# Hash products in one two-bank PSUM tile, values scaled before they are split, loads with a first allowed time

## The chip, the cores and the metric

The kernel runs on one NeuronCore of one Trainium2 chip. The metric is the device time of one execution in microseconds (us), taken from several runs of the same program; lower is better. A profile is one further execution with the hardware profiler on. Five engines work side by side, each with its own instruction queue that is worked off in order: PE (matrix products), ACT (activations, copies, casts), DVE (vector operations), POOL (vector operations, SBUF only) and SP, which here issues nearly all DMAs.

## The reference

Two batches of eight heads, 768 tokens, head size 64. Attention is masked by a hash: six projections of q and of k are turned into sign bits, and a query sees the keys whose six bits equal its own. The result goes through two feed-forward networks with different gates.

```python
q_bits = (np.einsum('bhsd,dk->bhsk', q, proj) > 0)      # proj: 64 x 6
k_bits = (np.einsum('bhsd,dk->bhsk', k, proj) > 0)
mask = q_bucket[:, :, :, None] == k_bucket[:, :, None, :]
scores = np.where(mask, scale * q @ k^T, -1e9)
attn = softmax(scores)
x = (attn @ v)                       # 1536 tokens x 512
h = x @ w_in1;  x = (h * sigmoid(h)) @ w_out1            # 512 -> 2048 -> 512
h = x @ w_in2;  x = (h - tanh(h)) @ w_out2
```

## The kernel before, in words

**Precision.** Each fp32 product is built from two parts, a rounded high part and a low rest, so a product is three matmuls (high*high, high*low, low*high). Casting to the high part and subtracting to get the low part is most of the work of ACT, DVE and POOL.

**Attention.** There are 16 heads (numbers 0 to 15; 0 to 7 are batch 0) with 6 query tiles of 128 rows each, 96 tiles in all. For a head, a raw tile `r` with q and k is loaded (L372), split into `q1, q2, k1, k2` (L380 to L396), and the hash products go into PSUM (`hash_mm`, L413): two halves of 384 tokens, each into a bank of its own taken from the three to four general banks (`banks`). DVE turns the products into bit rows: for head 0 four instructions that write straight into the operands (`ev0`, L423), for every other head two instructions into a helper tile `hb` (`ev`, L437), from which SP copies the rows by two DMAs (L445, L448) into the operands, where they act as extra rows of the score product, so that a mismatch pushes a score far down.

For a tile: scores (PE, L558) into a two-bank PSUM tile out of `s_slots`, of which there are two until batch 0 is through and one after that; row maximum and eviction (DVE, L562); bias (L567); exp (ACT, L572); then the transpose of the probabilities, in one of two ways. A *direct* tile is transposed by PE in two halves (L586), each evicted into fp16 high (ACT, L595) and low (DVE, L599) parts. Any other tile is cast to fp16 (ACT, L614), its rest is subtracted on POOL (L617), and the pair is transposed by a DMA issued from SP (L620) into `pt`. The knobs `direct` and `direct1` say which share of the tiles of batch 0 and batch 1 is direct: 0.4 and 0.083, which gives 19 and 4 tiles. Then the product with the values (PE, L635 to L637, 18 matmuls).

**Values.** For each batch six row blocks are loaded in three DMAs (L461) and scanned for the largest magnitude (`v_max`, L470, DVE); one PE product spreads it over all partitions (L480), and a power of two `vsc` comes out (L483 to L487). `v_hi` (ACT, L502) writes the scaled fp16 high part, and `v_lo` the rest: one DVE instruction that scales and subtracts (L512), or two on POOL. No value product may start before all twelve pieces are done. The raw values of both batches use the same SBUF slot (`acc_slot`), so the loads of batch 1 wait for the last `v_lo` of batch 0.

**Feed-forward.** Weights are loaded as 64-bit floats, 512 KB a piece (L799), and turned into fp32 on the chip: `c_abs` (ACT), `c_clip` (L834, POOL or DVE), three DVE instructions (L837, L841, L845), a cast (ACT, L849) and a subtraction (L853). Converted weights of the first network are also stored to DRAM (L872) for a second pass. The first network's tokens of batch 0 run interleaved with the attention of batch 1; then come the first network's second half and the second network with seven products in place of eight (L1229) and its output product (L1321). Its weight conversion has the same steps (L1084 to L1105).

**The order.** The order of every queue is written out before the program is built. `Plan.add` takes an engine (or several, with a price for each), a key (a due time) and dependencies; `Plan.order` (L95) is a list scheduler over assumed prices: it takes the work that could start first, and among work within `slack` of that the one with the lowest key. A task with a second or third engine goes there when that would end earlier by more than a bias (`b_...`; 50 or more means never). Keys come from `when(i)` (L330), which gives tile i the time `start + step * i` in batch 0 and a gap and `step1` in batch 1, and from `t_group` for the feed-forward products. A DMA without unmet dependencies may be placed as soon as SP is free in the plan. On the chip each queue runs in the planned order whatever the real durations are: an instruction that is not ready holds up all behind it.

Of the kernel before, what the change touches and what calls it, by code (L numbers as in the profile page):

```python
# [23 lines left out]

KNOBS = dict(start=1.134, step=2.53, gap=9.388, step1=3.92, ffn=3.61, ffn3=2.212, pv=12.257, prep=16.11, hash=8.464,
             slack=0.042, conv=32.734, conv0=53.318, vld=10.124, vmax=13.049, vsplit=16.427, x2=0.269, direct=0.4,
             direct1=0.083, b_qh=1.32, b_qlo=100, b_kup=100, b_vlo=2, b_bi=2.75, b_thi=100, b_shi=0.98, b_slo=100,
             b_xh=1.72, b_xlo=1.56, b_wlo=100, b_clip=-0.24, b_hhi=0.67, k_m=-0.273, k_e=0.107, k_t=1.899,
             k_th=2.064, k_tl=2.019, k_hi=1.332, k_lo=1.98, k_f=3.209, cj=3.559, cl=8.822, ahead=2, emode=1, lmode=1,
             xsets=0, raws=5, vmax1=70.287, ffn2=2.15, xprep=14.912, xprep1=2.896, xk1=2.806, convo=54.917,  # L30
             convh=37.499, fill=14.668, convo0=35.195, convh0=75.173, fill0=45.82, plain=3, cj2=5.837, half=2,
             b_xph=1.92, b_xpl=-0.35, b_cl2=2.16, b_wl2=100, b_sh=100, b_ss=1.98, b_u3=100, b_hh2=1.76, b_hl2=-0.24,
             by=3.547)

# [19 lines left out]
class Task:  # L54
    __slots__ = ("ways", "eng", "fn", "key", "deps", "uses", "takes", "left", "next", "ready", "end", "start", "tail",
                 "opens", "n", "bias", "line")


class Plan:
# [7 lines left out]

    def add(self, eng, cost, fn, key, deps=(), takes=(), uses=(), tail=0.0, port=False, give=None, line=None):
# [17 lines left out]
        t.next, t.end, t.start = [], None, None  # L86
        t.n = len(self.tasks)
        self.tasks.append(t)
        return t
# [113 lines left out]
def lsh_attention_moe_kernel(  # L203
# [116 lines left out]
    def get(h):  # L320
        if h.tile is None:
            h.tile = h.slots[0].make()
        return h.tile
# [35 lines left out]
    for n in range(NHEAD):  # L359
# [47 lines left out]
        if n >= THREE:  # L407
            parts.append(add(("ACT", "POOL", "DVE"), (0.82, 1.84, 0.6), k_up, at + 1, [ld[1], hold], uses=[raw, ops],
                             port=("DVE",), give="kup"))
        hk = [Held(*banks), Held(*banks)]  # L410
        hat = a0 - K["hash"] if n else -45.0

        def hash_mm(n=n, hk=hk, get_ops=get_ops):  # L413
            q1, q2, k1, k2 = get_ops()
            for u in range(2):
                pairs = ((hq1, q1), (hk1, k1), (hk2, k2), (hq2, q2)) if n < THREE else ((hq1, q1), (hk1, k1), (hqk, q2))
                for i, (w, x) in enumerate(pairs):
                    nc.tensor.matmul(out=get(hk[u])[0:82, 0:HS], lhsT=w, rhs=x[:, u * HS:(u + 1) * HS],  # L418
                                     start=(i == 0), stop=(i == len(pairs) - 1))

        hm = add("PE", 1.4 if n < THREE else 1.05, hash_mm, hat, parts + [hash_ready], takes=hk, uses=[ops])
        if n == 0:
            def ev0(u, side, hk=hk, get_ops=get_ops):  # L423
                _, q2, _, k2 = get_ops()
                us = slice(u * HS, (u + 1) * HS)
                ps = get(hk[u])[0:82, 0:HS]
                if side == 0:
                    nc.vector.tensor_scalar(q2[0:18, us], ps[0:18, :], thr[0:18, :], sc[0:18, :],
                                            op0=ALU.is_gt, op1=ALU.mult)
                else:  # L430
                    nc.vector.tensor_scalar(k2[0:18, us], ps[64:82, :], thr[64:82, :], None, op0=ALU.is_gt)
            bits = [add("DVE", 0.64, lambda u=u, s=s: ev0(u, s), hat + 1, [hm], uses=[ops, hk[u]])
                    for u in range(2) for s in range(2)]
        else:
            hb = Held((hb_slot,))

            def ev(u, hk=hk, hb=hb):  # L437
                nc.vector.tensor_scalar(get(hb)[0:82, u * HS:(u + 1) * HS], get(hk[u])[0:82, 0:HS], thr[0:82, :],
                                        sc[0:82, :], op0=ALU.is_gt, op1=ALU.mult)
# [10 lines left out]
            bits = [add("SP", 0.73, f, hat + 2, [e0, e1], uses=[hb, ops], tail=0.18) for f in (bits_q, bits_k)]  # L450
        heads[n] = (ops, get_ops, bits)

    vals = {}
    for b in range(B):
# [5 lines left out]
        def load_v(t, b=b, vr=vr):  # L460
# [42 lines left out]

        def v_lo(e, t, vr=vr, vh=vh, vsc=vsc):
            row = get(vr)[:, t, :]
            src = row.rearrange("p (h d) -> p h d", h=H)
            hi, lo = (x[:, t, :, 0:D] for x in get(vh))
            if e == "POOL":
                nc.gpsimd.tensor_scalar(row, row, vsc, None, op0=ALU.mult)
                nc.gpsimd.tensor_tensor(lo, src, hi, op=ALU.subtract)  # L510
            else:
                nc.vector.scalar_tensor_tensor(lo, src, vsc, hi, op0=ALU.mult, op1=ALU.subtract)  # L512

        out = []
        for t in range(NQ):
            x = add("ACT", 0.72, lambda t=t, f=v_hi: f(t), a0 + K["vsplit"] + t, [t3, vo], uses=[vr, vh])
            out += [x, add(("DVE", "POOL"), (0.745, 2.6), lambda e, t=t, f=v_lo: f(e, t), a0 + K["vsplit"] + 0.5 + t, [x],
                           uses=[vr, vh], port=("DVE",), give="vlo")]
# [236 lines left out]
    for ps_i, (e, fresh, blks) in enumerate(PASSES):  # L755
        pairs = [blks[i:i + 2] for i in range(0, len(blks), 2)]
        accs = {}
        for c in range(NCH):
            base = seq[0]
            wset = []  # L760
            for m in range(2):
# [18 lines left out]
                for j in range(4):  # L780
# [16 lines left out]
                    def load_w(src=src, w_tile=w_tile, fresh=fresh):  # L797
# [3 lines left out]
                    ld = add("SP", 0.35, load_w, kj - K["cl"], ([] if fresh else [stored[ps_i - 1, c, m, j]]),  # L801
                             takes=[w], tail=1.65 if fresh else 0.82)
                    prior = [first_take] if first_take else [ld]
# [11 lines left out]
                    else:  # L815
# [252 lines left out]
    for c in range(NCH):  # L1068
        cb = unit0 + CU * c

        def fetch(m, j, wv, key):
# [20 lines left out]
            def c_clip(e):  # L1092
                ENG[e].tensor_scalar(val().bitcast(F32), val().bitcast(F32), W_MIN, W_MAX, op0=ALU.max, op1=ALU.min)  # L1093

# [12 lines left out]

            ld = add("SP", 0.35, load, key - K["cl"], [], takes=[w], tail=1.65)
            a = add("ACT", 0.65, c_abs, key, [ld, spare] + wv.first[:1], takes=[] if wv.first else [wv],
# [294 lines left out]
```

## Time and profile before

| | |
|---|---|
| median of 3 runs | 745.14 us (742.0 to 747.14) |
| the profiled execution | 746.36 us, span 744.6 us |
| PE busy | 704.2 us, 95% of the span, 5390 matmuls |
| DVE / ACT / POOL busy | 558.3 us / 452.2 us / 504.3 us |
| mean granted TensorE clock | 0.988 of full speed |

The span runs from the first to the last instruction of the profile; the rest of the execution's time lies around it. PE's busy time counts overlapping matmuls once and goes on while a matmul waits in the array, so a busy PE is not one at its peak. DMA share is the mean busy share of the 16 DMA engines and can come out slightly above 1. In rows "x <- y" reads "x was waited for by": the engine and line on the left stood idle until the one on the right was done. SPq is SP's queue.

### The profile page before, as it was taken

To read this page: it belongs to the slowest core of one execution; us is meant where nothing else is said; L and a number is where in the kernel's file an instruction comes from. 1 tells how busy PE (TensorE), PEld (TensorE's weight loads), DVE (VectorE), ACT (ScalarE), POOL (GpSimd) and SP (SyncE) were. 2 spreads that over 40 slices of the span, in tenths; PEclk is the share of its full clock that TensorE was granted. 3 is DMA by queue.
4 is the path that set the end of the run, shared out by engine and by line. 5 is a ranking of instruction groups with operands and counts; after the bars stand their busy time and mean duration, and the time that the engine had idled before them with its cause. 6 is when DMAs were issued, how large, how long until landed. Compare 5 with 4: busy or idle time off the path is not lost.

```text
span 744.6 us, 14192 instructions
## 1 busy us (share of the span) xinstructions
PE 704.2 (95%) x5390; PEld 679.6 (91%) x5390; DVE 558.3 (75%) x1025; ACT 452.2 (61%) x853; POOL 504.3 (68%) x340
## 2 busy tenths in 40 slices
PE   5679888799999999999999999989999999999998
PEld 4569787599999999999999999989999999999997
DVE  5889998798987888986834464888869768775453
ACT  5879998897796984875634344464535445253240
POOL 5757887679699874776942467897897598565120
PEclk9889999999999999999999999999999999999999
DMA  9687899979999997894322322312312202300102
GB/s 355 145 214 136 209 183 219 258 147 241 244 246 235 240 198 208 204 194 115 92 74 84 86 85 85 108 36 64 113 47 88 87 29 70 101 1 1 53 33 85
DMA packets 140447, 100.77 MB, mean 135 GB/s; under 512 B 117439, under 2 KB 119743, under 8 KB 140379
## 3 DMA queue, kind: packets, MB, share of 16 engines
q1 hardware_dynamic: 140090, 99.59, 54.0%
q8 instruction: 42, 0.69, 0.4%
q10 hardware_dynamic: 288, 0.28, 0.1%
q14 instruction: 27, 0.21, 0.1%
HBM read 57.95 MB, written 11.53 MB: 93 GB/s over the span
## 4 chain that ended last, share of the span: by engine, by line
PE 65%; ACT 9%; DVE 7%; POOL 7%; DMA 7%; issue 4%; SPq 0%; POOLq 0%; ACTq 0%; DVEq 0%
PE psm L1321 14%; PE psm L1229 13%; PE psm L906 13%; PE psm L968 11%; PE ps L558 6%; ACT p L572 2%; DMA w<-in_w_in_dram 2%; PE psm L418 2%; POOL wl L810 2%; POOL x L1093 2%; PE pso L635 2%; PE pso L636 1%; PE pso L637 1%; ACT hl L338 1%; DMA w<-in_w_out_dram 1%
## 5 line engine op out<-in xcount | busy, mean ns | idle before, releaser
L617 POOL TENSOR_TENSOR hl<-p,hl 128x768 f16<-128x768 f32 x73 | 121.5, 1666 | 54.7 <-ACT hl L338 42.6
L562 DVE TENSOR_SCALAR_CACHE_REDUCE p<-ps 128x768 f32<-128x768 f32 x96 | 90.4, 952 | 17.7 <-PE ps L558 11.1
L558 PE MATMUL ps<-k,q 128*128 128x384 f32 x384 | 90.7, 363 | 5.7 <-DVE p L562 3.9
L572 ACT ACTIVATE p<-p,bi 128x768 f32<-128x768 f32 x96 | 89.4, 937 | 1.8
L906 PE MATMUL psm<-xh,wh 128*128 128x384 f32 x256 | 86.9, 340 | 1.1 <-DVE p L599 0.7
L968 PE MATMUL psm<-gh,wh 128*128 128x384 f32 x256 | 86.7, 339 | 0.0
L906 PE MATMUL psm<-xl,wh 128*128 128x384 f32 x256 | 86.2, 337 | 0.2 <-DVE xl L677 0.2
L906 PE MATMUL psm<-xh,wl 128*128 128x384 f32 x256 | 86.1, 336 | 0.0
L968 PE MATMUL psm<-gh,wl 128*128 128x384 f32 x256 | 85.7, 335 | 0.0
L968 PE MATMUL psm<-gl,wh 128*128 128x384 f32 x256 | 85.7, 335 | 0.0
L1321 PE MATMUL psm<-gl,wh 128*128 128x384 f32 x256 | 85.6, 334 | 0.0
L1321 PE MATMUL psm<-gh,wh 128*128 128x384 f32 x256 | 85.5, 334 | 0.0
L1321 PE MATMUL psm<-gh,wl 128*128 128x384 f32 x256 | 85.5, 334 | 0.0
L558 PEld LDWEIGHTS ps<-k,q 128*128 128x128 f32 x384 | 67.4, 197 | 8.8 <-DVE p L562 4.6
L810 POOL TENSOR_TENSOR wl<-w,wh 128x512 fp32r<-128x512 f32 x32 | 44.6, 1403 | 37.1 <-ACT wh L806 37.0
L338 ACT CAST hl<-p 128x768 f16<-128x768 f32 x71 | 59.1, 833 | 0.5
L635 PEld LDWEIGHTS <-pt 128*128 128x128 f16 x438 | 40.0, 97 | 15.0 <-DMA pt<-hl 8.1
L635 PE MATMUL pso<-v,pt 128*128 128x65 f16 x438 | 47.8, 195 | 6.2 <-DMA pt<-hl 6.0
L1328 DVE TENSOR_TENSOR acc<-acc,psm 128x384 f32<-128x384 f32 x48 | 26.4, 551 | 33.3 <-PE psm L1321 33.1
L853 POOL TENSOR_TENSOR wl<-wa,wh 128x512 fp32r<-128x512 f32 x32 | 42.1, 1317 | 12.2 <-ACT wh L849 11.9
L924 DVE TENSOR_TENSOR gl<-psm,gh 128x384 fp32r<-128x384 f32 x64 | 35.2, 553 | 19.6 <-ACT gh L338 19.1
L906 PEld LDWEIGHTS psm<-xh,wh 128*128 128x128 f32 x256 | 48.1, 188 | 1.9 <-DVE p L599 1.2
(146 smaller groups left out, 2222.3 us busy)
## 6 DMA issues: line engine op xcount, KB each, us to landing
w<-in_w_in_dram SPq DMA_DIRECT2D x32, 512.0 KB
w<-in_w_out_dram SPq DMA_DIRECT2D x32, 512.0 KB
r<-in_qkT_dram SPq DMA_DIRECT2D x15, 768.0 KB
wi<-wa SPq DMA_DIRECT2D x16, 256.0 KB
wo<-wa SPq DMA_DIRECT2D x16, 256.0 KB
w<-wi SPq DMA_DIRECT2D x16, 256.0 KB
w<-wo SPq DMA_DIRECT2D x16, 256.0 KB
vr<-in_v_dram SPq DMA_DIRECT2D x6, 512.0 KB
```

Source lines behind the costliest of these rows:

```text
L338: nc.scalar.copy(out, in_) if e == "ACT" else ENG[e].tensor_copy(out, in_)
L558: nc.tensor.matmul(out=get(ps)[:, u, 0:HS], lhsT=x[:, t * 128:(t + 1) * 128], rhs=c[:, u * HS:(u + 1) * HS], start=(j == 0), stop=(j == 1))
L562: nc.vector.tensor_scalar(get_p().rearrange("p (c s) -> p c s", c=2), get(ps)[:, :, 0:HS], FLOOR, None, op0=ALU.max, op1=ALU.max, accum_ou ...
L572: nc.scalar.activation(out=get_p(), in_=get_p(), func=ACTF.Exp, scale=0.125, bias=get(bi))
L617: ENG[e].tensor_tensor(get_hl()[:, 1, :], get_p(), get_hl()[:, 0, :], op=ALU.subtract)
L635: nc.tensor.matmul(out=o, lhsT=pt[:, kt, :], rhs=v16[:, kt, h, :], start=(kt == 0), stop=False)
L810: ENG[e].tensor_tensor(ll, w_tile(), hh.bitcast(F32), op=ALU.subtract)
L853: ENG[e].tensor_tensor(ll, get(wa).bitcast(F32), hh.bitcast(F32), op=ALU.subtract)
L906: nc.tensor.matmul(out=ps, lhsT=a[:, k, fs], rhs=b_[blk][:, k, :], start=(k == 0 and j == 0), stop=(k == KD - 1 and j == 2))
L968: nc.tensor.matmul(out=ps, lhsT=a[:, f, ds], rhs=b_.tile[:, f, :], start=(f == 0 and j == 0), stop=(f == F - 1 and j == 2))
L1229: nc.tensor.matmul(out=ps, lhsT=sw[a][:, o, 2 * k + p, :], rhs=xw[b_][:, k, :], start=(first and k == 0 and j == 0), stop=(k == 1 and j == 2),
L1321: nc.tensor.matmul(out=ps, lhsT=a[:, f, ds], rhs=b_.tile[:, f, :], start=(f == 0 and j == 0), stop=(f == F - 1 and j == 2))
```

## The change

Five things are edited. (a) The hash products of a head go into one two-bank tile out of `s_slots`, and one DVE instruction of 768 columns takes the place of the two (heads from 2 on); heads 0 and 1 (`near=2`) write their bit rows straight into the operands, in two instructions of 768 columns, without helper tile and copies. (b) DVE multiplies a row block of the values by the scale in place (fp32), after `v_hi` has read it, and `v_lo` is then a plain subtraction, on POOL (its bias is 100). (c) `add` gets `hold`, a first allowed time in the plan: for the raw tiles from head 2 on, for the values of batch 0, and for the weight loads. (d) `c_clip` has its minimum ahead of its maximum. (e) All knobs have new values; among them `direct1` is 0.02, so that one tile of batch 1 is direct instead of four.

```diff
+KNOBS = dict(start=1.018, step=2.297, gap=9.393, step1=3.658, ffn=3.741, ffn3=2.596, ..., prep=14.861,
+             hash=8.525, ..., conv0=69.778, vld=10.109, vmax=14.731, vsplit=16.895, ..., direct=0.4, direct1=0.02,
+             b_qh=100, ..., b_kup=1.56, b_vlo=100, ..., raws=6, ..., hold_r=30, hold_v=21.393, hold_v1=0.554,
+             hold_w=10.342, hold_o=57.604, near=2)
...
-            t.ready = 0.0
+            t.ready = t.hold
...
-                      takes=[raw], tail=2.47)] * 2
+                      takes=[raw], tail=2.47, hold=at - K["hold_r"] if n > 1 else 0.0)] * 2
...
-        hk = [Held(*banks), Held(*banks)]
+        hk = Held(*one(s_slots))
...
-        if n == 0:
-            def ev0(u, side, hk=hk, get_ops=get_ops):
+        if n < K["near"]:
+            def ev0(side, hk=hk, get_ops=get_ops):
...
+            bits = [add("DVE", 1.03, lambda s=s, f=ev0: f(s), hat + 1, [hm], uses=[ops, hk]) for s in range(2)]
...
-            e0 = add("DVE", 0.665, lambda ev=ev: ev(0), hat + 1, [hm], takes=[hb], uses=[hk[0]])
-            e1 = add("DVE", 0.665, lambda ev=ev: ev(1), hat + 1, [hm, e0], uses=[hk[1], hb])
+            def ev(hk=hk, hb=hb):
+                nc.vector.tensor_scalar(get(hb)[0:82, :].rearrange("p (u s) -> p u s", u=2), get(hk)[0:82, :, 0:HS],
+                                        thr[0:82, :], sc[0:82, :], op0=ALU.is_gt, op1=ALU.mult)
+            e0 = add("DVE", 1.03, ev, hat + 1, [hm], takes=[hb], uses=[hk])
...
-        ld = [add("SP", 0.5, lambda t=t, f=load_v: f(t), la + 0.1 * t, [begin], uses=[vr], tail=1.65)
+        ld = [add("SP", 0.5, lambda t=t, f=load_v: f(t), la + 0.1 * t, [begin], uses=[vr], tail=1.65,
+                  hold=K["hold_v"] + t * K["hold_v1"] if b == 0 else 0.0)
...
-                nc.vector.scalar_tensor_tensor(lo, src, vsc, hi, op0=ALU.mult, op1=ALU.subtract)
+        def v_scaled(t, vr=vr, vsc=vsc):
+            nc.vector.tensor_scalar(row, row, vsc, None, op0=ALU.mult)
...
+            ENG[e].tensor_tensor(lo, src, hi, op=ALU.subtract)
...
+            y = add("DVE", 0.4, lambda t=t, f=v_scaled: f(t), a0 + K["vsplit"] + 0.3 + t, [x], uses=[vr], port=True)
+            out += [x, add(("POOL", "DVE"), (1.29, 0.72), lambda e, t=t, f=v_lo: f(e, t), a0 + K["vsplit"] + 0.5 + t, [y],
                            uses=[vr, vh], port=("DVE",), give="vlo")]
...
-                             takes=[w], tail=1.65 if fresh else 0.82)
+                             takes=[w], tail=1.65 if fresh else 0.82, hold=kj - K["cl"] - K["hold_o" if ps_i else "hold_w"])
...
-                            ENG[e].tensor_scalar(lead(), lead(), W_MIN, W_MAX, op0=ALU.max, op1=ALU.min)
+                            ENG[e].tensor_scalar(lead(), lead(), W_MAX, W_MIN, op0=ALU.min, op1=ALU.max)
```

## Rows read from the trace of the kernel before

**Rows 1.** Busy time by stretch: PE, PEld, DVE, ACT, POOL, then clock, DMA share, GB/s.

```profile
10.00:60.00 50.00, 38.21 (x337) 33.56 (x336) 41.41 (x83) 38.46 (x67) 34.09 (x21) 0.86 0.76 211
60.00:110.00 50.00, 45.78 (x643) 41.98 (x641) 47.23 (x107) 49.91 (x98) 40.26 (x25) 1.00 0.97 187
110.00:150.00 40.00, 31.30 (x357) 25.74 (x354) 33.40 (x71) 34.36 (x66) 30.24 (x22) 1.00 1.03 230
150.00:340.00 190.00, 190.00 (x1792) 182.42 (x1791) 165.12 (x314) 147.92 (x269) 147.21 (x93) 1.00 0.95 216
480.00:540.00 60.00, 56.69 (x314) 55.48 (x313) 51.81 (x83) 31.67 (x62) 51.40 (x34) 0.97 0.25 80
```

**Rows 2.** The chain that ended last: start, length, what (matmuls; a weight load's transfer).

```profile
350.31 16.64 PE psm L906 x96
...
510.19 3.65 DMA w<-in_w_in_dram
```

**Rows 3.** Idle time of ACT by what ended it, 10 to 60 us.

```profile
ACT bi L567 <- DVE p L562: 3.7, 4, 2.6
ACT p L338 <- PE psm L586: 3.4, 4, 1.4
ACT v L502 <- DVE vsc L487: 2.6, 1, 2.6
```

**Rows 4.** Idle time by what ended it, 0 to 150 us.

```profile
PEld L635 <- DMA pt<-hl: 8.0, 7, 3.4
...
ACT wa L831 <- DMA w<-in_w_out_dram: 3.0, 1, 3.0
...
ACT wa L831 <- DMA wo<-wa: 2.0, 2, 1.3
```

**Rows 5.** DVE's groups by line, 10 to 60 us: busy us, mean ns.

```profile
L562 DVE TENSOR_SCALAR_CACHE_REDUCE p<-ps 128x768 f32<-128x768 f32 x17 | 16.0, 952 | 3.0 <-PE ps L558 2.8
L512 DVE SCALAR_TENSOR_TENSOR v16l<-vr,vsc,v 128x512 f16<-128x512 f32 x6 | 4.9, 858 | 0.0
L438 DVE TENSOR_SCALAR hb<-psm,cst_sb 82x384 fp32r<-82x384 f32 x6 | 4.0, 671 | 0.8 <-DMA k<-hb 0.4 <-PE psm L418 0.3
L428 DVE TENSOR_SCALAR q<-psm,cst_sb 18x384 fp32r<-18x384 f32 x2 | 1.3, 666 | 1.4 <-PE psm L418 1.3
L431 DVE TENSOR_SCALAR k<-psm,cst_sb 18x384 fp32r<-18x384 f32 x2 | 1.2, 612 | 0.0
```

**Rows 6.** One line at a time: durations min/median/max in ns over the whole run.

```profile
L512 DVE SCALAR_TENSOR_TENSOR v16l<-vr,vsc,v x12: 742/747/2119, 32.2 to 159.5; 128x512 f16<-128x512 f32 x12
...
L834 DVE TENSOR_SCALAR wa<-wa x15: 417/665/1781, 108.8 to 315.4; 128x512 f32<-128x512 f32 x15
...
L853 POOL TENSOR_TENSOR wl<-wa,wh x32: 1274/1292/1487, 50.1 to 330.4; 128x512 fp32r<-128x512 f32 x32
...
L1093 POOL TENSOR_SCALAR wa<-wa x16: 1910/1916/2639, 409.2 to 640.2; 128x512 f32<-128x512 f32 x16
```

**Rows 7.** The timeline of SP's queue, 0 to 50 us.

```profile
2.64 2.86 SPq L461 DMA_DIRECT2D vr<-in_v_dram  x3
5.54 0.94 SPq L799 DMA_DIRECT2D w<-in_w_in_dram  x2
...
38.73 0.90 SPq L461 DMA_DIRECT2D vr<-in_v_dram  x2
```

**Rows 8.** SP's queue, 20 to 60 us: what its issue waited for.

```profile
SPq L461 <- DVE v16l L512: 7.6, 1, 7.6
```

**Rows 9.** The timeline of PE, 290 to 296 us: the six transposes of a direct tile, then scores.

```profile
293.49 0.82 PE L586 MATMUL psm<-cst_sb,p 128*128 128x128 f32 x6
294.06 0.95 PE L558 MATMUL ps<-k,q 128*128 128x384 f32 x4
```

**Rows 10.** Idle time of PE by what ended it, 150 to 745 us.

```profile
PE psm L1229 <- ACT x L1239: 2.5, 2, 1.9
PE psm L1229 <- DVE psm L1245: 1.8, 2, 0.9
```

**Rows 11.** The timeline, 22 to 38 us: the value scan's last group, the first value product.

```profile
22.73 1.86 DVE L470 TENSOR_REDUCE vm<-vr 128x1 f32<-128x512 f32 x3
...
37.56 0.10 PEld L635 LDWEIGHTS <-pt 128*128 128x128 f16 x1 [0.16 <-issue]
```

More of the change, by code (lines that the diff above doesn't have):

```diff
@@ L23 @@
 W_MAX = 2.0 ** 16 * (1.875 - 2.0 ** -23)
[L25 to L33, printed above, removed]
+KNOBS = dict(start=1.018, step=2.297, gap=9.393, step1=3.658, ffn=3.741, ffn3=2.596, pv=12.257, prep=14.861,
+             hash=8.525, slack=0.056, conv=34.996, conv0=69.778, vld=10.109, vmax=14.731, vsplit=16.895, x2=0.271,
+             direct=0.4, direct1=0.02, b_qh=100, b_qlo=100, b_kup=1.56, b_vlo=100, b_bi=2.87, b_thi=100, b_shi=100,
+             b_slo=100, b_xh=0.41, b_xlo=-0.2, b_wlo=100, b_clip=1.08, b_hhi=0.67, k_m=-0.273, k_e=0.537, k_t=1.776,
+             k_th=2.388, k_tl=2.072, k_hi=1.332, k_lo=1.987, k_f=3.209, cj=3.089, cl=8.317, ahead=2, emode=1,
+             lmode=1.209, xsets=0, raws=6, vmax1=71.495, ffn2=1.548, xprep=14.965, xprep1=2.616, xk1=2.807,
+             convo=53.113, convh=41.45, fill=12.117, convo0=35.089, convh0=78.247, fill0=48.895, plain=3, cj2=5.285,
+             half=2, b_xph=100, b_xpl=-0.35, b_cl2=1.82, b_wl2=2.89, b_sh=100, b_ss=2.39, b_u3=100, b_hh2=0.86,
+             b_hl2=-0.24, by=3.983, hold_r=30, hold_v=21.393, hold_v1=0.554, hold_w=10.342, hold_o=57.604, near=2)
 class Slot:
@@ L55 @@
     __slots__ = ("ways", "eng", "fn", "key", "deps", "uses", "takes", "left", "next", "ready", "end", "start", "tail",
-                 "opens", "n", "bias", "line")
+                 "opens", "n", "bias", "line", "hold")
 class Plan:
@@ L66, in __init__, with add @@
         self.lines = {}
-    def add(self, eng, cost, fn, key, deps=(), takes=(), uses=(), tail=0.0, port=False, give=None, line=None):
+    def add(self, eng, cost, fn, key, deps=(), takes=(), uses=(), tail=0.0, port=False, give=None, line=None, hold=0.0):
         t = Task()
@@ L85, in add @@
             self.lines[line] = t.line[1] + 1
-        t.next, t.end, t.start = [], None, None
+        t.next, t.end, t.start, t.hold = [], None, None, hold
         t.n = len(self.tasks)
@@ L417, in hash_mm @@
                 for i, (w, x) in enumerate(pairs):
-                    nc.tensor.matmul(out=get(hk[u])[0:82, 0:HS], lhsT=w, rhs=x[:, u * HS:(u + 1) * HS],
+                    nc.tensor.matmul(out=get(hk)[0:82, u, 0:HS], lhsT=w, rhs=x[:, u * HS:(u + 1) * HS],
                                      start=(i == 0), stop=(i == len(pairs) - 1))
-        hm = add("PE", 1.4 if n < THREE else 1.05, hash_mm, hat, parts + [hash_ready], takes=hk, uses=[ops])
-        if n == 0:
-            def ev0(u, side, hk=hk, get_ops=get_ops):
+        hm = add("PE", 1.4 if n < THREE else 1.05, hash_mm, hat, parts + [hash_ready], takes=[hk], uses=[ops])
@@ L424, in ev0 @@
+        if n < K["near"]:
+            def ev0(side, hk=hk, get_ops=get_ops):
                 _, q2, _, k2 = get_ops()
-                us = slice(u * HS, (u + 1) * HS)
-                ps = get(hk[u])[0:82, 0:HS]
+                ps = get(hk)[64:82, :, 0:HS] if side else get(hk)[0:18, :, 0:HS]
                 if side == 0:
-                    nc.vector.tensor_scalar(q2[0:18, us], ps[0:18, :], thr[0:18, :], sc[0:18, :],
+                    nc.vector.tensor_scalar(q2[0:18, :].rearrange("p (u s) -> p u s", u=2), ps, thr[0:18, :], sc[0:18, :],
@@ L429, in ev0 @@
                                             op0=ALU.is_gt, op1=ALU.mult)
                 else:
-                    nc.vector.tensor_scalar(k2[0:18, us], ps[64:82, :], thr[64:82, :], None, op0=ALU.is_gt)
-            bits = [add("DVE", 0.64, lambda u=u, s=s: ev0(u, s), hat + 1, [hm], uses=[ops, hk[u]])
-                    for u in range(2) for s in range(2)]
+                    nc.vector.tensor_scalar(k2[0:18, :].rearrange("p (u s) -> p u s", u=2), ps, thr[64:82, :], None,
+                                            op0=ALU.is_gt)
@@ L448, in bits_k @@
                 nc.sync.dma_start(out=get_ops()[3][0:18, :].bitcast(F32), in_=get(hb)[64:82, :].bitcast(F32))
-            bits = [add("SP", 0.73, f, hat + 2, [e0, e1], uses=[hb, ops], tail=0.18) for f in (bits_q, bits_k)]
+            bits = [add("SP", 0.73, f, hat + 2, [e0], uses=[hb, ops], tail=0.18) for f in (bits_q, bits_k)]
         heads[n] = (ops, get_ops, bits)
@@ L502, in v_hi, with v_lo @@
             nc.scalar.activation(out=get(vh)[0][:, t, :, 0:D], in_=src, func=ACTF.Copy, scale=vsc)
-        def v_lo(e, t, vr=vr, vh=vh, vsc=vsc):
+        def v_scaled(t, vr=vr, vsc=vsc):
             row = get(vr)[:, t, :]
-            src = row.rearrange("p (h d) -> p h d", h=H)
+            nc.vector.tensor_scalar(row, row, vsc, None, op0=ALU.mult)
+        def v_lo(e, t, vr=vr, vh=vh):
+            src = get(vr)[:, t, :].rearrange("p (h d) -> p h d", h=H)
             hi, lo = (x[:, t, :, 0:D] for x in get(vh))
[L508 to L511, printed above, removed]
-                nc.vector.scalar_tensor_tensor(lo, src, vsc, hi, op0=ALU.mult, op1=ALU.subtract)
+            ENG[e].tensor_tensor(lo, src, hi, op=ALU.subtract)
         out = []
@@ L1092, in c_clip @@
             def c_clip(e):
-                ENG[e].tensor_scalar(val().bitcast(F32), val().bitcast(F32), W_MIN, W_MAX, op0=ALU.max, op1=ALU.min)
+                ENG[e].tensor_scalar(val().bitcast(F32), val().bitcast(F32), W_MAX, W_MIN, op0=ALU.min, op1=ALU.max)
             def c_shift():
@@ L1106, in c_low @@
                                                op0=ALU.logical_shift_right, op1=ALU.bitwise_or)
-            ld = add("SP", 0.35, load, key - K["cl"], [], takes=[w], tail=1.65)
+            ld = add("SP", 0.35, load, key - K["cl"], [], takes=[w], tail=1.65, hold=key - K["cl"] - K["hold_o"])
             a = add("ACT", 0.65, c_abs, key, [ld, spare] + wv.first[:1], takes=[] if wv.first else [wv],
```

4 lines of the change are left out of this document (removed).

## The prediction

> **What bounds the kernel now.** I first read the busy time by stretch, to see where PE idles. From 150 to 340 us PE is busy for all of it, so there only less PE work counts; before that it idles 11.8 us of 50, 4.2 of 50 and 8.7 of 40, and in 480 to 540 us another 3.3 [rows 1]. The chain of waits agrees: from 350 us on whole stretches of it are PE alone, 96 matmuls in 16.64 us, 173 ns each [rows 2]. The feed-forward work cannot start before the attention of batch 0 is through, at about 150 us, and it then keeps PE full. So the time is set by how long the first 150 us take, by the amount of PE work behind them, and by a few gaps.
>
> What bounds the first stage is read from the other engines in the same rows. From 60 to 110 us ACT is busy 49.91 us of 50: it is the limit there and nothing of the change relieves it. From 10 to 60 us ACT idles 11.5 us, and DVE is the busiest of the three vector engines (41.4 us) [rows 1]. Most of that idle time has a name: 3.7 us for the row maxima of DVE, 2.6 us for the value scale that DVE makes, 3.4 us for transposes of PE [rows 3]. From 110 to 150 us ACT idles 5.6 us at a DMA share of 1.03 [rows 1], and 5.0 us of that are waits for a weight load and for a weight store [rows 4]. The value products, too, wait 8.0 us for DMA transposes in the first 150 us [rows 4].
>
> **The change, part by part.** *Hash products in one step.* An eviction of 768 columns for 82 partitions is not in the trace. Nearest is the score eviction, also two banks and 768 columns: 952 ns. The bound above is no gain, two at 671 ns, 1.34 us [rows 5]. I take 0.95 us: the columns are the same. That is 0.39 us less of DVE for each head from 2 on. Head 0 goes from 2 x 0.666 + 2 x 0.612 = 2.56 us to two of 0.95, 0.66 less [rows 5]. Head 1 goes from 1.34 us to 1.90, 0.56 more, but loses two copies on SP. Three heads are evicted from 10 to 60 us after head 0 (six instructions, [rows 5]), so the opening has 0.66 - 0.56 + 2 x 0.39 = 0.9 us less of DVE. Later savings lie beside a full ACT or a full PE and count nothing. The products now take one of the two score tiles for about 2.5 us a head. The next scores have the other: 0.8 us of PE and 0.95 us of DVE a tile are less than ACT's two microseconds a tile, so I cost that at nothing; with no second tile free it would cost up to those 2.5 us once a head. After the switch to one score tile PE is full with other work, which hides it.
>
> *Values.* Six instructions of L512 took 4.9 us in the opening, 747 ns at the median and 2119 ns at worst [rows 5, 6]. In their place DVE gets six one-input fp32 instructions of 512 columns, nearest the clip on DVE: 417 ns at least, 1781 ns at most [rows 6]. With 0.42 us six are 2.5 us, 2.4 less; with 1.78 us they are 10.7 us, 5.8 more. I take the lower end, as POOL idles 15.9 us in this stretch [rows 1]. POOL gets six subtractions of 1.29 us [rows 6], 7.7 us in a row, where the six of DVE took 6.5 us with score evictions among them; that delays the first value product by 1.3 us, bounds 0 and 7.7.
>
> The stretching of the DVE clip from 417 to 1781 ns is the row that speaks against this edit [rows 6]. The Trainium skill, SBUF — State Buffer, "SBUF: two separate sides", says that DVE in a two-port mode and POOL take a shared port pair as an exclusive lock, held for the whole instruction. By that rule each scaling could stand behind one POOL instruction, and the sum would be 8.2 us longer; the spread in the trace agrees with it, but the least value shows it does not always happen.
>
> *Held loads.* SP issued the value loads at 2.64 us and two weight loads at 5.54 us, ahead of any work on them being due [rows 7]. Held, the values start at 21.4 us of the plan's time and the weights shortly before their conversion. This takes transfers and two weight conversions out of the opening. What SP lost there is seen once: 7.6 us in which it stood at the value loads of batch 1, which need the slot that the last L512 frees, with the transposes of two tiles queued behind [rows 7, 8]. That load has no hold in the new code either. I cannot work out the new order; bounds for opening and order together are nothing and all of ACT's 11.5 us. I take half, **5.7 us**, in which the DVE terms (0.9 + 2.4) are contained. From 110 to 150 us the same: bounds are a further wait of 3.0 us, as the one that stands there, and the gain of 5.0 us [rows 4]; I take half of the gain, **2.5 us**, since raw tiles and weights are then no longer issued long ahead of the transposes.
>
> *Direct tiles.* Three tiles of batch 1 leave PE's transposes. One such tile is 0.57 us of PE from its start to the next product's [rows 9], where PE is full: **1.7 us** less. They get a cast on ACT instead of two half evictions, a subtraction on POOL and a DMA transpose, in a stretch with a DMA share of 0.95 [rows 1]; the bound above is no gain.
>
> *Clip and prices.* The clip with its operations exchanged costs what it did, 1916 ns on POOL [rows 6]; the bounds are that and the 1.29 us of a subtraction. It bears only on the late gaps, whose waits of PE are 4.3 us in all [rows 10]; new keys and biases may close or double them. I take nothing, bounds 4.3 us either way.
>
> **The sum.** 5.7 + 2.5 + 1.7 = 9.9 us. The profiled execution took 746.4 us (span 744.6), so 736.5 us; the median of the runs is 1.2 us lower, which gives **735 us**.
>
> **Rivals.** *The order gives nothing* (the queues stand at other waits for as long): only the PE term stays, 745.1 - 1.7 = 743 us. For it: ACT has a full load from 60 us on whatever DVE saves. Against it: the opening's idle time has DVE and SP as its causes, both of which the change touches.
>
> *All of ACT's idle time goes*: 11.5 + 5.0 + 1.7 = 18.2 us, 727 us, and 723 us with the late gaps closed. Against it: the start of the pipeline always leaves some.
>
> *The port*: the scalings wait for POOL, the opening is 8.2 us worse than forecast, 743 us. The Trainium skill's rule of the shared port pair (the section named above) would make it so.
>
> *The values come too late*, the case on the other side. The last scan of the values ended at 24.6 us and the first value product began at 37.56 us [rows 11], 13.0 us later. With the third load held to 21.39 + 4 x 0.554 = 23.6 us, a transfer of 3.65 us as for a weight piece of the same size [rows 2] and one scan of 0.67 us, the scan ends at 27.9 us, and the first product comes at 27.9 + 13.0 + 1.3 = 42.2 us, 4.6 us later than now. Until then the tiles fill all buffers and ACT stops. If the delay is paid once, 748 us; if SP also stands the longer at the loads of batch 1, twice, 753 us, and a clock that falls as it did here (0.86 from 10 to 60 us, [rows 1]) adds to it, 756 us. It decides from a first value product later than about 41 us. Against it: the scan and the scale wait for DVE and PE now, not for the loads, and with the opening relieved they may take less than 13 us.
>
> **How the numbers follow.** Within 1% is 737.7 to 752.6 us; about that much can be told from no change. Forecast 0.43 (own range 729 to 741 us: between a fifth and nine tenths of the two ACT terms), all idle time gone 0.14 (723 to 729), order gives nothing 0.24 and the port 0.04 (739 to 748), values too late 0.15 (747 to 757). Faster by over 1%: most of the forecast, 0.37, and 0.14, about 0.52. Slower: two thirds of the last case and a little for a late gap that doubles, 0.12. The rest, 0.36, is within 1%. The range that holds 8 in 10 leaves out the ends of the two outer cases: 722 to 750 us.
>
> **What would show it.** Right: ACT idles under 6 us from 10 to 60 us and PE is full from about 140 us; hash evictions of 0.95 us on DVE, scalings near 0.42 us, six fewer transposes for each of three tiles. Wrong in the steps: scalings near 1.8 us (the port); a first value product after 41 us and PE full only after 150 us (values too late); PE full from 148 us as now, with the waits for transposes unchanged (the order gives nothing). The forecast fails most easily in its two halves of ACT's idle time, which are chosen between bounds and not worked out.

## The result, and the profile after

The changed kernel takes 736.09 us (median of 6 runs, 734.99 to 737.39) beside 743.1 us of the kernel before on the same chip (6 runs, 741.97 to 747.14): ratio 0.990, 95% interval 0.987 to 0.993. The profiled execution has a span of 734.4 us, 10.2 us less than before.

The forecast of 735 us was met, but most of the time came from a place where the prediction had written nothing. Two marks in the trace show it: the start of the long unmixed block of the first network (96 matmuls of L906 in a row, [rows 2]) and the first product of the second network (L1229).

| | before | after | difference |
|---|---|---|---|
| first long block of L906 | 350.3 us | 347.2 us | -3.2 |
| first product L1229 | 483.3 us | 480.1 us | -3.2 |
| end of the span | 744.6 us | 734.4 us | -10.2 |
| from the first L1229 to the end | 261.3 us | 254.3 us | **-7.0** |

So the opening and the whole mixed part gave 3.2 us, and the second network 7.0 us. The table compares single executions: the profiled one of before took 746.36 us, 3.3 us more than the median of its runs, that of after lay on its median (736.15 us). The medians differ by 7.0 us, not 10.2, and in which stretch the 3.3 us lie is not known; runs 1 and 2 below rest on the medians too.

Busy time by stretch of the kernel after, columns as in [rows 1]:

```profile
10.00:60.00 50.00, 36.16 (x318) 29.37 (x317) 44.14 (x81) 38.84 (x70) 37.49 (x26) 0.90 0.77 205
60.00:110.00 50.00, 44.77 (x609) 39.33 (x606) 48.05 (x104) 48.29 (x94) 41.07 (x28) 1.00 1.03 220
110.00:150.00 40.00, 35.27 (x425) 31.44 (x424) 35.47 (x74) 38.38 (x76) 34.73 (x26) 1.00 1.04 244
150.00:340.00 190.00, 188.44 (x1777) 180.52 (x1776) 158.42 (x300) 145.36 (x259) 138.80 (x97) 1.00 0.97 214
480.00:540.00 60.00, 60.00 (x347) 60.00 (x346) 50.91 (x82) 32.71 (x63) 45.03 (x36) 1.00 0.22 71
```

Against [rows 1], ACT's idle time from 10 to 60 us is what it was (11.2 us, 11.5 before); from 110 to 150 us it fell from 5.6 to 1.6 us. But add up PE's idle time over the four stretches to 340 us: 11.8 + 4.2 + 8.7 + 0 = 24.7 us before, 13.8 + 5.2 + 4.7 + 1.6 = 25.4 us after. What the third stretch gained the others lost. The 3.2 us are therefore less busy time of PE and not less waiting. The last row is the one that moved: PE full and the clock at 1.00, where 56.69 of 60 and 0.97 stood before.

The chain of waits says why. First that of before, 473 to 502 us (start, length, what), a part that the prediction's rows did not hold:

```profile
473.79 1.89 POOL x L1093
475.68 1.82 POOL xl L1017
477.50 1.89 POOL x L1093
...
483.71 2.60 POOL wa L1093
488.25 0.83 ACT xh L338
490.15 0.83 ACT xth L338
491.42 11.04 PE psm L1229 x54
```

The same view of the kernel after:

```profile
463.63 16.64 PE psm L968 x96
480.27 14.73 PE psm L1229 x84
```

PE alone now, and POOL's share of the whole chain fell from 7% to 1%. The line that stood in it is the clip of the second network, L1093, 1916 ns an instruction in [rows 6]. One line of the kernel after, minimum/median/maximum in ns:

```profile
L1093 POOL TENSOR_SCALAR x<-x x16: 614/617/631, 405.4 to 641.5; 128x512 f32<-128x512 f32 x16
L1093 POOL TENSOR_SCALAR wa<-wa x14: 605/617/871, 388.8 to 633.0; 128x512 f32<-128x512 f32 x14
```

Exchanging the two operations of that instruction made it three times as fast. How a slow clip on POOL reached PE is in the timeline of before, 482 to 494 us (start, length, engine, line; in brackets the idle time ahead and what ended it):

```profile
483.66 4.52 POOL L1093 TENSOR_SCALAR wa<-wa 128x512 f32<-128x512 f32 x2
...
486.33 0.69 DVE L1096 TENSOR_SCALAR cv<-wa 128x512 int32<-128x512 int32 x1 [1.35 <-POOL wa L1093]
...
487.67 0.55 DVE L975 TENSOR_TENSOR acc<-acc,psm 128x384 f32<-128x384 f32 x1
...
488.25 0.83 ACT L338 CAST xh<-acc 128x768 fp32r<-128x768 f32 x1 [2.46 <-DVE acc L975]
...
488.99 0.47 ACT L1239 COPY x<-psm 128x384 f32<-128x384 f32 x1
...
489.51 0.44 PE L1229 MATMUL psm<-xh,wh 128*128 128x384 f32 x1 [1.87 <-ACT x L1239]
```

Read it upwards. PE waits 1.87 us for a copy of ACT. PE's last matmul before it had ended at 487.6 us, but the copy stands in ACT's queue behind a cast, which waits 2.46 us for DVE's L975. That stands in DVE's queue behind L1096 and the next step of the same weight (L1101, 487.06 to 487.75 us); L1096 waits for POOL's clip, the first of the two at 483.66 us. Three queues in order hand the clip's length on. DVE's waits for the clip from 400 to 660 us, in us, times and longest, are in before:

```profile
DVE cv L1096 <- POOL wa L1093: 15.6, 10, 2.9
DVE cv L1096 <- POOL x L1093: 7.8, 9, 1.9
```

After the change neither is left. Of the 7.0 us, 4.3 are the waits of [rows 10]. In before the granted clock of 490 to 500 us was 0.83, after PE had stood still for 1.87 us; a part of those 10 us ran at the lower of its two levels, 1.2 GHz, where after the change all of it is at 2.4 GHz. That is 0.17 x 10 = 1.7 us, an estimate. In the rows of L1229 one matmul lasts 0.34 us and the next starts 0.17 us after it, so each of the four waits costs about 0.17 us more than the idle time, 0.7 us in all. The last 0.3 us I cannot assign.

### The profile page after: what moved, and what is told of

Read it like the earlier page. It is cut to its first block, busy times and chain, and to the rows that moved or that the text cites. A ratio compares the mean times of both kernels' runs of the same rounds, so it can differ in the third digit from the quotient of the medians.

```text
span 734.4 us, 14154 instructions
## 1 busy us (share of the span) xinstructions
PE 698.0 (95%) x5372; PEld 672.6 (92%) x5372; DVE 557.1 (76%) x1011; ACT 451.3 (61%) x843; POOL 459.8 (63%) x354
## 4 chain that ended last, share of the span: by engine, by line
PE 80%; ACT 8%; DVE 4%; DMA 4%; issue 2%; POOL 1%; SPq 0%; DVEq 0%; ACTq 0%; POOLq 0%
PE psm L1321 18%; PE psm L968 17%; PE psm L906 17%; PE psm L1229 16%; PE ps L558 6%; ACT p L572 3%; DMA pt<-hl 2%; PE pso L635 2%; PE ps L419 1%; PE pso L636 1%; PE pso L637 1%; ACT hl L339 1%; ACT p L339 1%; DVE p L562 1%; DMA r<-in_qkT_dram 1%
## 5 line engine op out<-in xcount | busy, mean ns | idle before, releaser
L617 POOL TENSOR_TENSOR hl<-p,hl 128x768 f16<-128x768 f32 x76 | 126.5, 1667 | 46.7 <-ACT hl L339 37.3
L906 PE MATMUL psm<-xh,wh 128*128 128x384 f32 x256 | 86.9, 340 | 0.0
L906 PE MATMUL psm<-xh,wl 128*128 128x384 f32 x256 | 86.1, 336 | 0.0
L906 PE MATMUL psm<-xl,wh 128*128 128x384 f32 x256 | 86.1, 336 | 0.0
L339 ACT CAST hl<-p 128x768 f16<-128x768 f32 x76 | 63.2, 835 | 0.7
L1328 DVE TENSOR_TENSOR acc<-acc,psm 128x384 f32<-128x384 f32 x48 | 26.4, 552 | 43.9 <-PE psm L1321 43.9
L635 PEld LDWEIGHTS <-pt 128*128 128x128 f16 x456 | 42.0, 98 | 11.8 <-issue 8.9
L635 PE MATMUL pso<-v,pt 128*128 128x65 f16 x456 | 50.6, 196 | 1.7 <-DMA pt<-hl 1.5
L636 PE MATMUL pso<-v16l,pt 128*128 128x65 f16 x456 | 50.0, 195 | 0.0
L637 PE MATMUL pso<-v,pt 128*128 128x65 f16 x456 | 49.8, 194 | 0.0
L975 DVE TENSOR_TENSOR acc<-acc,psm 128x384 f32<-128x384 f32 x48 | 26.4, 551 | 30.8 <-PE psm L968 30.5
```

Source lines behind the costliest of these rows:

```text
L339: nc.scalar.copy(out, in_) if e == "ACT" else ENG[e].tensor_copy(out, in_)
L617: ENG[e].tensor_tensor(get_hl()[:, 1, :], get_p(), get_hl()[:, 0, :], op=ALU.subtract)
L635: nc.tensor.matmul(out=o, lhsT=pt[:, kt, :], rhs=v16[:, kt, h, :], start=(kt == 0), stop=False)
L636: nc.tensor.matmul(out=o, lhsT=pt[:, kt, :], rhs=v16l[:, kt, h, :], start=False, stop=False)
L637: nc.tensor.matmul(out=o, lhsT=pt[:, NQ + kt, :], rhs=v16[:, kt, h, :], start=False, stop=(kt == NQ - 1))
L906: nc.tensor.matmul(out=ps, lhsT=a[:, k, fs], rhs=b_[blk][:, k, :], start=(k == 0 and j == 0), stop=(k == KD - 1 and j == 2))
```

## Experiments

Times are medians; the second time of each pair is the kernel before, measured on the same chip beside the run. Its median lies between 743.1 and 745.62 us in the different sets, so two runs are compared by their ratios to it; 0.01 is 7.4 us.

**1. The clip alone** (the kernel before, every queue in its old order).

```diff
-  ENG[e].tensor_scalar(lead(), lead(), W_MIN, W_MAX, op0=ALU.max, op1=ALU.min)
+  ENG[e].tensor_scalar(lead(), lead(), W_MAX, W_MIN, op0=ALU.min, op1=ALU.max)
...  # the same at L1093
```

> The kernel before with one edit: the clip has its minimum ahead of its maximum, in both weight conversions. The order of all queues is that of before. Theory (the cheaper clip on POOL closes the late gaps): POOL's clip falls from 1916 to about 617 ns, the stretch from the first product of the second network to the end falls from 261 us to about 255, and the time from 743 to 736 or 737 us. Rival (the new keys and biases of the late stage close the gaps): the clip gets cheaper and the time stays within 1 us of 743.

737.09 us against 744.23: ratio 0.990, 0.988 to 0.992. This is the whole ratio of the change. Its row for 480 to 540 us and its clip:

```profile
480.00:540.00 60.00, 60.00 (x346) 60.00 (x345) 51.30 (x83) 32.40 (x63) 43.32 (x36) 1.00 0.21 71
...
L1093 POOL TENSOR_SCALAR wa<-wa x16: 605/614/618, 407.4 to 632.8; 128x512 f32<-128x512 f32 x16
```

The first L1229 starts at 481.9 us and the span ends 254.3 us later, the same 254.3 us as in the whole change. The long block of L906 starts 1.4 us earlier than before, so against the one profiled execution of before the clip is worth 7.0 us late and 1.4 us earlier, 8.4 us of span; in medians it is 7.1 us.

**2. The clip put back** (the kernel after, its order kept).

```diff
-  ..., W_MAX, W_MIN, op0=ALU.min, op1=ALU.max)
+  ..., W_MIN, W_MAX, op0=ALU.max, op1=ALU.min)     # both places
```

> The changed kernel with the clip in its old order (maximum first), all else kept. Theory (the clip closes the late gaps): the last stretch gets 6 to 7 us longer again, 742 to 743 us. Rival (the new keys and biases close them): within 1 us of 736.

742.62 us against 744.23: ratio 0.9975, 0.9959 to 0.9990. All of the change but the clip gives a quarter of a per cent. Its profiled execution was the fastest of its twelve (740.45 us), so its span is only 4.3 us above that of after, 1.8 us of it from the first L1229 on, where the ratios put the clip at 5.6 us; but the difference is of the same kind: POOL's clips are in the chain again, and PE idles from 480 to 540 us.

```profile
480.00:540.00 60.00, 58.77 (x336) 57.95 (x335) 51.87 (x82) 32.12 (x62) 53.28 (x36) 1.00 0.24 78
...
480.67 2.60 POOL wa L1093
485.21 0.84 ACT xh L339
487.15 0.83 ACT xth L339
488.42 9.66 PE psm L1229 x54
```

Both directions agree, at unchanged order: the clip is the cause of the gain.

**3. Instructions by themselves**, in a small kernel without the attention and the networks: the two clip orders, single operations, and DVE's scaling beside POOL's subtraction, 128x512 each.

```diff
+    ts = nc.gpsimd.tensor_scalar
+    for _ in range(4):
+        ts(o, b, W_MIN, W_MAX, op0=ALU.max, op1=ALU.min)
+    for _ in range(4):
+        ts(o, b, W_MAX, W_MIN, op0=ALU.min, op1=ALU.max)
...
+    for _ in range(6):
+        nc.gpsimd.tensor_tensor(l, a, h, op=ALU.subtract)
+        nc.vector.tensor_scalar(d, d, s, None, op0=ALU.mult)
```

> No attention and no feed-forward: POOL's two-operation instruction on 128x512 fp32 alone, four times each, with maximum first and with minimum first, on a constant inside the bounds and on the values (half of them below the lower bound), then single operations and a multiply-add; then DVE's in-place scaling alone, beside POOL's subtraction, and the old single instruction beside it. If the order of the two operations sets POOL's price: 1.9 us for maximum first and 0.6 us for minimum first on both inputs. If the data do: the two inputs differ and the orders don't. If DVE and POOL shut each other out: scalings of 0.42 us alone and over 1 us beside POOL; the old instruction the same, or 0.75 us as alone.

One line each, minimum/median/maximum in ns. In order: maximum then minimum, minimum then maximum, maximum alone, multiply and add, POOL's subtraction; then DVE's scaling (L73) and the old scale-and-subtract (L78) beside POOL's subtraction, and L82, the latter alone.

```profile
L49 POOL TENSOR_SCALAR o<-b x4: 1913/1914/1925, 3.1 to 9.1; 128x512 f32<-128x512 f32 x4
L51 POOL TENSOR_SCALAR o<-b x4: 612/612/613, 11.1 to 13.2; 128x512 f32<-128x512 f32 x4
L57 POOL TENSOR_SCALAR o<-a x4: 1484/1484/1487, 24.6 to 29.3; 128x512 f32<-128x512 f32 x4
L61 POOL TENSOR_SCALAR o<-a x4: 617/617/617, 37.2 to 39.3; 128x512 f32<-128x512 f32 x4
L65 POOL TENSOR_TENSOR l<-a,h x4: 1151/1212/1214, 46.5 to 50.3; 128x512 f16<-128x512 f32 x4
...
L73 DVE TENSOR_SCALAR d<-d,s x6: 714/1255/1369, 56.3 to 62.4; 128x512 f32<-128x512 f32 x6
L78 DVE SCALAR_TENSOR_TENSOR l<-d,s,h x6: 752/1250/1633, 64.8 to 71.4; 128x512 f16<-128x512 f32 x6
L82 DVE SCALAR_TENSOR_TENSOR l<-d,s,h x6: 744/752/752, 72.4 to 76.3; 128x512 f16<-128x512 f32 x6
```

The clip's price is a property of the instruction, 1914 against 612 ns, not of its neighbours. It does not depend on the data either: on the loaded values in place of a constant the two orders take the same 1914 and 612 ns (L53 and L55, not shown). Durations on POOL are rough, but the starts agree: the first and the fourth of L49 start 6.0 us apart, those of L51 2.1 us. And a DVE instruction on SBUF beside a subtraction of POOL lasts 1250 ns, about as long as one such subtraction (1212 ns), whether it has one input tile or two. The scaling alone was not obtained here: the six meant for it (L68, 715 to 1369 ns) ran beside subtractions too.

**4. The hash part alone** (the kernel before with part (a)).

```diff
-        hk = [Held(*banks), Held(*banks)]
+        hk = Held(*one(s_slots))
...
+            e0 = add("DVE", 1.03, ev, hat + 1, [hm], takes=[hb], uses=[hk])
```

> The kernel before with the hash products in one two-bank tile and one eviction, heads 0 and 1 straight into the operands; old knobs, old values, old clip. Theory (DVE is relieved by 0.3 us a head where ACT or PE has a full load): eviction 1.06 us, time within 2 us of 743. Rival (the opening's DVE work sets the end of the first stage): 2 to 4 us faster, 739 to 741. A rival on the other side: the hash products take a score tile and the scores wait, 2 to 4 us slower.

750.20 us against 744.23: ratio 1.008, 1.007 to 1.010, slower.

**5. The values part alone** (the kernel before with part (b)).

```diff
+            y = add("DVE", 0.4, ... v_scaled ..., [x], uses=[vr], port=True)
+            out += [x, add(("POOL", "DVE"), (1.29, 0.72), ... v_lo ..., [y], ...)]
```

> The kernel before with the values scaled in place by DVE and subtracted on POOL, and the key of the split moved by 0.47 us to its new value; all else as before. Theory (DVE's scaling and POOL's subtraction hold each other up): the scalings take about 1 us each instead of 0.42 in the opening, the first value product comes 3 to 8 us later than 37.6 us, and the time is 0 to 5 us longer, 743 to 748. Rival (DVE is relieved, as the prediction had it): 1 to 3 us shorter.

757.70 us against 744.23: ratio 1.017, 1.015 to 1.020, slower; the first value product came at 45.3 us. Runs 4 and 5 look like strong verdicts against their parts. They are not: the list scheduler wrote a new order for the whole program in each, and run 9 shows what that alone does.

**6. The values part taken back** from the kernel after, with a new order.

```diff
-            nc.vector.tensor_scalar(row, row, vsc, None, op0=ALU.mult)
...
+                nc.vector.scalar_tensor_tensor(lo, src, vsc, hi, op0=ALU.mult, op1=ALU.subtract)
```

> The changed kernel with the values split as before: one DVE instruction scales and subtracts, no POOL; all else as changed. Theory (the scalings on DVE and the subtractions on POOL shut each other out from 38.6 to 46.8 us, and PE stands 5.8 us behind them): the first value product comes at about 43 us instead of 47.0, and the time is 2 to 5 us shorter, 731 to 734 us. Rival (ACT is full from 60 us on and takes the gain back): within 1 us of 736. Rival on the other side (the keys were chosen with the new split): 2 to 6 us longer.

743.99 us against 744.46: ratio 0.999, 0.997 to 1.001. The first value product came at 39.7 us, 7.3 us earlier than after, and by the ratios the kernel was some 6.5 us slower.

**7. The values not held, and 8. the weights held less** (the kernel after, new orders).

```diff
-  hold_v=21.393, hold_v1=0.554, hold_w=10.342
+  hold_v=0, hold_v1=0, hold_w=10.342         # 7
+  hold_v=21.393, hold_v1=0.554, hold_w=30    # 8
```

> The changed kernel with no first allowed time for the values of batch 0; weights and raw tiles are held as changed. Theory (the hold makes the value scan late, which costs little as the scan waits for DVE anyway): the loads go out in the first 10 us again, the first value product comes 3 to 8 us earlier than 47.0 us, the time is within 2 us of 736. Rival (the early value loads push back the raw tiles of the next heads): 2 to 5 us longer. Rival (values too late was a real price): 2 to 5 us shorter.

> The changed kernel with the weights' first allowed time 30 us ahead of their due time in place of 10.3; all else as changed. Theory of the prediction (weight loads issued early stand in front of DMA transposes and take ACT and DVE in the opening): 1 to 4 us longer, 737 to 740. Rival (the holds do nothing that the in-order queues don't undo): within 1 us of 736.

Run 7: 753.67 us against 744.46, ratio 1.011, 1.008 to 1.015; first value product at 42.8 us. Run 8: 747.15 us, ratio 1.003, 1.001 to 1.006.

**9. An order for control**: the kernel after, the same instructions, only the assumed price of the score eviction one per cent higher in the planner.

```diff
-            m = add("DVE", 1.03, soft_max, ...)
+            m = add("DVE", 1.04, soft_max, ...)
```

> The changed kernel with one price in the planner altered by a hundredth (1.04 us in place of 1.03 for the score eviction); no operation, hold or key differs, only the order that the planner writes. It tells how far the last three experiments measured their edit. If the order alone, unmatched to the knobs, costs what they cost: 5 to 15 us longer than 736, all in the first pass, with the late stretch at 254 us. If those edits were the cause themselves: within 2 us of 736.

750.78 us against 745.62: ratio 1.008, 1.005 to 1.010. The order alone costs some 13 us against the kernel after, by the ratios 1.008 and 0.990. So no run with a new order (4 to 8, 10 and 11) tells what its edit costs, in either sign.

One thing those runs do tell, since it holds whatever the order: the time from the first L1229 to the end.

| kernel | clip | first L1229 | from there to the end |
|---|---|---|---|
| before | old | 483.3 | 261.3 |
| 4, hash part alone | old | 489.2 | 260.8 |
| 5, values part alone | old | 495.0 | 261.0 |
| 2, clip put back | old | 482.6 | 256.1 |
| after | new | 480.1 | 254.3 |
| 1, clip alone | new | 481.9 | 254.3 |
| 6, values taken back | new | 488.2 | 254.6 |
| 7, values not held | new | 497.7 | 254.2 |
| 8, weights held less | new | 491.6 | 254.3 |
| 9, order for control | new | 495.0 | 254.2 |
| 10, clip and direct tiles | new | 487.4 | 254.4 |
| 11, clip priced | new | 495.5 | 255.2 |
| 12, values back, order kept | new | 480.8 | 254.3 |

With the new clip it is 254.2 to 255.2 us, with the old one 256.1 (run 2, in its fastest execution) to 261.3. Two rows for 480 to 540 us, the values part alone (old clip) and the order for control (new clip), each with the start of L1229 (first and last, after the durations):

```profile
480.00:540.00 60.00, 57.19 (x319) 56.42 (x318) 51.48 (x82) 29.98 (x56) 50.69 (x32) 0.97 0.23 80
...
L1229 PE MATMUL psm<-xh,wh x128: 332/336/522, 495.0 to 735.0; 128*128 128x384 f32 x128
```

```profile
480.00:540.00 60.00, 60.00 (x347) 60.00 (x346) 52.24 (x84) 31.86 (x59) 41.59 (x35) 1.00 0.25 84
...
L1229 PE MATMUL psm<-xh,wh x128: 334/337/342, 495.0 to 728.2; 128*128 128x384 f32 x128
```

Both start at 495.0 us, and the second ends the second network's products 6.8 us earlier (735.0 against 728.2).

**10. Clip and fewer direct tiles, 11. the new clip with its true price in the planner**; both were tries at a kernel better than either.

```diff
+  direct1=0.02                                        # 10: before + clip
+  add(("POOL", "DVE"), (0.62, 0.42), c_clip, ...)     # 11: after, 1.29 -> 0.62
```

> The kernel before with the clip exchanged and the direct share of batch 1 at 0.02, so three tiles more go through DMA transposes; all else as before. Theory of the prediction (1.7 us of PE work less where PE is full): 735 to 736 us, 1.7 below the clip alone. Rival (the new order of batch 1 costs as much or more): 737 us or longer.

> The changed kernel with the planner told what POOL's clip now takes: 0.62 us in place of 1.29. More clips go to POOL and DVE gets room. Theory (a truer price gives a better order): 1 to 3 us faster, 733 to 735. Rival (any order but the one the knobs were chosen with is worse): 740 to 750 us.

Run 10: 744.13 us against 745.62, ratio 0.998, 0.996 to 1.000, by the ratios some 6 us worse than the clip alone. Run 11: 751.36 us, ratio 1.008, 1.006 to 1.011. Both lost to their new orders; a truer price gave a worse order here.

**12. The values part taken back, order kept.** In the kernel after, DVE's scaling step issues the old single instruction and POOL's subtraction step issues nothing.

```diff
-            nc.vector.tensor_scalar(row, row, vsc, None, op0=ALU.mult)
+            nc.vector.scalar_tensor_tensor(lo, src, vsc, hi, op0=ALU.mult, op1=ALU.subtract)
...
-            ENG[e].tensor_tensor(lo, src, hi, op=ALU.subtract)
+            pass
```

> The kernel after, its order on every queue kept, but the two steps that split a batch of values are put together again: VectorE's step, at its old place in the queue, is the one instruction of before (scale and subtract, fp32 with fp16 to fp16), and GpSimd's six subtractions of a batch are gone. Theory (GpSimd's subtraction beside VectorE's scaling is what made the second batch last 7.6 us and the first value product start at 47.0): the six instructions take about 0.75 us each, v16l is there some 3 us earlier, the first value product starts at about 43 to 44, TensorE's wait of 5.8 us on the hash eviction shrinks, and the kernel takes 731 to 735 us. Rival (the opening's time is taken back later by ScalarE, or by the weights that SyncE holds back): the first value product comes earlier and the whole stays within 1 us of 736. The other side: SyncE's order was laid for the old lengths, and it stays above 737.

736.88 us (6 runs, 736.21 to 738.93) against 744.07: ratio 0.991, 0.988 to 0.994, not to be told from the change's own. First the timeline of the kernel after, 36 to 52 us:

```profile
38.61 5.92 DVE L506 TENSOR_SCALAR vr<-vr,vsc 128x512 f32<-128x512 f32 x6
...
39.22 7.62 POOL L511 TENSOR_TENSOR v16l<-vr,v 128x512 f16<-128x512 f32 x6
...
45.57 1.65 PE L558 MATMUL ps<-k,q 128*128 128x384 f32 x4 [5.80 <-DVE hb L438]
...
48.37 1.65 PE L558 MATMUL ps<-k,q 128*128 128x384 f32 x4
```

and the same of this kernel:

```profile
38.92 4.07 DVE L508 SCALAR_TENSOR_TENSOR v16l<-vr,vsc,v 128x512 f16<-128x512 f32 x6 [0.15 <-ACT v L502]
...
44.03 1.65 PE L558 MATMUL ps<-k,q 128*128 128x384 f32 x4 [4.18 <-DVE hb L438]
...
44.98 1.46 DVE L834 TENSOR_SCALAR wa<-wa 128x512 f32<-128x512 f32 x1 [1.01 <-ACT wa L831]
...
47.08 0.95 DVE L562 TENSOR_SCALAR_CACHE_REDUCE p<-ps 128x768 f32<-128x768 f32 x1
...
48.09 1.65 PE L558 MATMUL ps<-k,q 128*128 128x384 f32 x4 [1.40 <-DVE p L562]
```

The stall beside POOL is real and the one instruction removes it: six take 4.07 us instead of 5.92, PE's wait shrinks from 5.80 to 4.18 us, and the scores come 1.54 us earlier. One group of scores later the lead is 0.28 us. DVE now stands 1.01 us at a weight conversion that waits for ACT, and the next score eviction is queued behind it. The rival was right: what the opening gains is taken back within 4 us, by ACT's place in the order. No kernel tried beats the change by more than the runs can tell.

## Why the prediction was right and wrong

**The number was right, the place was not.** The sum was 5.7 + 2.5 + 1.7 from the first half and nothing from the second network; the traces have 3.2 and 7.0. That the time came out is luck: 6.7 us too much in one place and 7.0 us too little in the other. In medians the gain was 7.0 us and not 9.9; the forecast started from 745.1 us over three runs, and over six the kernel before takes 743.1 us, which made up 2 us of the difference.

**The step that failed most** is "the clip with its operations exchanged costs what it did ... I take nothing, bounds 4.3 us either way". The clip went from 1916 to 617 ns, beyond the lower bound of 1290 ns. No row of before had the other order of operations, but that was no reason for a bound at a subtraction: DVE's clip of the same size stood at 417 ns in [rows 6], and a gain of all the late gaps was inside the prediction only as half of a rival. Runs 1 and 2 show 7.1 and 5.6 us for it. That is more than the 4.3 us of the bounds, too: a wait of PE also cost the restart behind it and a stretch at the lower clock. The step before it had failed too: "from 350 us on whole stretches of it are PE alone" is true of the row that was shown and was taken for the rest. The chain from 401 to 491 us ran through POOL, and the waits of [rows 10] name ACT and DVE only because a row names the last releaser; two steps further back stands L1093.

**The opening, 5.7 us of ACT's idle time, did not come.** ACT idles 11.2 us of 50 as before. The parts: the hash eviction takes 1.065 us, not 0.95, and with the two heads that write directly (1.065 and 1.012 us a side) 0.3 us is left of the 0.9. The values' scalings take 5.92 us where 2.5 were taken, and 4.9 stood before. The argument for the lower end, that POOL idles 15.9 us in that stretch, was empty, because the change itself puts six subtractions of POOL beside them: over the run a scaling lasts 477 to 1340 ns. The Trainium skill, SBUF — State Buffer, "SBUF: two separate sides", says that a DVE instruction in a two-port mode, or with two SBUF inputs, and one of POOL take their shared port pair as an exclusive lock, held for a whole instruction. The trace of run 3 agrees, with 1255 ns for a scaling beside a subtraction of 1212 ns.

**The port as a rival** had its mechanism right and its price wrong: it said 8.2 us of the kernel's time, and run 12 shows 1.5 us on the spot and nothing at the end.

**Values too late** was to decide from a first value product after 41 us. It came at 47.0 us and nothing of the rival's 748 to 756 us followed. With an order that has other work for PE and ACT there, the time of that product says little: 39.7 us in run 6, 45.5 in run 12, 47.0 after, with 743.99, 736.88 and 736.09 us.

**110 to 150 us** gave 4.0 us of ACT's time where 2.5 were taken, and 4.0 us of PE's; but PE's idle time up to 340 us was no less than before (25.4 against 24.7 us), so this was moved, not won. (The reading that the feed-forward work starts at about 150 us was wrong as well: the first L906 starts at 124.1 us before and 123.9 us after, so PE had such work in this stretch already.) **Direct tiles**: 18 transposes fewer (120 of L586, 138 before), 1.7 us forecast. The long block of L906 starts at 347.2 us after and at 348.9 us with the clip alone, 1.8 us, which fits but shows nothing by itself: other parts differ too, and a kernel with this edit and the clip alone (run 10) has another order.

**Order gives nothing**, the rival at 743 us, is nearly what the change does without its clip: 742.62 us in run 2, against 744.23 us. Whether the parts (a), (b) and (c) each do nothing or cancel each other stays open. Only run 12 takes one of them out at an unchanged order, and there the answer is nothing.

## What to carry to other kernels

Where the chain of waits was read in one place, read it over the whole span before calling a stretch "PE alone", and follow a wait of PE back through the queues: the engine that a row names may itself stand behind an instruction of a third engine. Price an exchanged operation as unknown on the engine that runs it, and run that edit alone first. In a program whose order comes from a list scheduler, test an edit with the order frozen; a new order moved this kernel by some 13 us, more than any edit.

## What the runs showed of the hardware that was not expected

On POOL, a 128x512 fp32 instruction of two operations costs 1914 ns as maximum then minimum and 612 ns as minimum then maximum; multiply and add costs 617 ns. A single maximum costs 1484 ns, more than twice the fast pair. The Trainium skill, GPSIMD Engine Reference, "4.1 Engine selection", calls one-input work on this engine roughly line-rate. By these rows that depends on the operations and their order (DVE's clip took 417 ns at best, [rows 6]), and the measurement decides.

DVE's old scale-and-subtract is stretched by a POOL subtraction as much as the new scaling is, from 752 to 1250 ns at the median. In the kernel before it took 742 ns at best and 2119 ns at worst [rows 6].
